# A planned attention-and-GLU kernel on one core: dummy key products in TensorE's rests, three head groups' row sums moved to VectorE, and new order tables

## The chip, the cores and the metric

The kernel runs on one core of a Trainium2 chip. The metric is device time in microseconds of the whole program; of several runs the median counts. One further execution was profiled, and everything below that is called the profile or the trace comes from it.

## The reference

Sequence length 2048, width 1024, 32 query heads of width 32 that share one key head and one value head, and a gated feed-forward part of width 3584. All tensors are bfloat16.

```python
x = A_x
h = x + attention(layernorm(x))       # q = xn@wq (32 heads), k = xn@wk, v = xn@wv (one head)
                                      # softmax(q k^T / sqrt(32)) v, heads side by side, @ wo
g, u = layernorm(h) @ w_gate, layernorm(h) @ w_up
out = h + (sigmoid(g) * u) @ w_down
```

## The kernel before

**Attention.** Scores are made in 512 *bursts* of four matmuls (L846 `s_burst`). Each of the four uses another 32-row strip of TensorE's array, so the four run at once; together they write 128 keys x 2048 query-head columns into four banks of PSUM (`S_ps`, three pairs of banks). ScalarE reads each half of a burst with one exponential (L866, 1024 columns, 1024 of them in the program) and writes it to a ring of tiles in SBUF (`Pr`; at first also to columns of `QT` and to `wo`, which are free then). Burst k may start when exponential 2k-2 has left its bank. Eight bursts cover 1024 keys for one query tile of 128 rows and 16 heads, and are a *group* (g). Two groups make all 2048 keys, and four groups make a query tile. The first 64 bursts (8 groups, tiles 0 and 1) are the *head*: meanwhile the layer norm of all 16 tiles, their transposes (DMA, L599) and the products for k, v and q are still being made.

For each group TensorE multiplies the probabilities with V (L953 `pv_group`, eight slots of four matmuls on 32-column strips) into one of only two banks, `X_ps`. The row sums of a group come in one of two ways (`SUM_PLAN`). With "p", TensorE multiplies all eight tiles with ones (L1015, eight slots). With "d", VectorE first adds the tiles pairwise (L903, L915: 14 adds of 128x1024), and TensorE multiplies only the sum with ones (L1000, one slot). Groups 0 to 7 have a letter each in `SUM_PLAN`; later groups are "d", only the last two bursts of all are added by L1015. Then VectorE transposes, inverts and multiplies (L1048 to L1058), which gives the attention output of the tile.

**The rest.** `wo_group` (projection and residual), second layer norm, and then the feed-forward part in eight *units* of two tiles: gate and up products (weights streamed from HBM in halves of 512 KB by SyncE's queue), a tanh on ScalarE (L1280) for the sigmoid, their product on VectorE (L1302), and the down products (`zone,hact` in the rows) with `w_down` kept in SBUF. Unit c runs while the scores of later tiles run; the last unit has nothing left to run beside.

**Three ways to use the array.** A product outside the scores is issued either as one matmul on all 128 columns (L368, mode "f") or as four at once on 32-column strips (L370, mode "pv"). Scores use row strips (mode "s"). In the rows below `128*128`, `128*32` and `32*128` are the three modes. `by_columns` chooses between "f" and "pv" for a product so as to keep the mode that the array is in; it refuses "pv" when too many instructions (`I_MAX`) were issued in the last 4 us.

**What sets the order.** All instructions of all engines are written by one Python loop, once, before launch. It keeps a clock for each engine (`k_pe`, `k_dve`, ...), adds estimated costs to it, and issues the next burst as soon as its clock says that the exponential is done (`due`), and otherwise products: of `todo` (k, v and the first q), `q_list`, `wo_list`, `ffn_list`, and P V groups by the letters of `PV_PLAN`. When nothing is ready it moves the clock on by 0.02 to 0.05 us and looks again; on the chip TensorE then waits at its next instruction. The tables (`TODO`, `PV_PLAN`, `Q_PLAN`, `LN_LEAD`, ...) steer these choices; they move instructions but do not change what is computed. The clock's estimates are not used for any time in this document.

```python
def run_item(g):                              # one product of a group
    if g.bank is None:
        ...
        need(pe, *after)                      # TensorE waits for the operands
        open_group(g)                         # and for one of the two X_ps banks
    mode("pv" if g.kind == "f" and by_columns(g) else g.kind)

def s_burst(k):
    g, b = BURST[k]
    t, i = ORDER[g]
    mode("s")
    need(pe, (c_e, 2 * k - 1) if k > 0 else None, *s_ready(k), ...)

def spare_dve():                              # may a q product of q_list or Q2 be started?
    return len(xn_val) >= min(NT, int(LN_LEAD + LN_RATE * k[0]))
```

Of the kernel before, what the change touches and what calls it, by code (L numbers as in the profile page):

```python
# [12 lines left out]
P = 128  # L13
# [73 lines left out]
def bass_sequential_preLN__grouped_kv_mqa__glu_gated_glu__prompt_kernel(  # L87
# [18 lines left out]
    NQ = D // P  # L106
# [13 lines left out]
    U_PLAN = "56391274"  # L120
    PV_PLAN = "aDcBBBaaDAaAeaabaDaAabaaaBaBDaaaabaDbbaaaAaAAcAaaBaAaaAaBCbDBadbaEDaDDaB"
    WO_PLAN = "aabbbaab"
    PV_HOLD = 1.5
# [3 lines left out]
    LN_LEAD = 1  # L127
    LN_RATE = 0.35
    T_PLAN = "aaadadad"
    H_ROOM = 0.2  # L130
    Q_PLAN = "daadddddddddddddddddddadddddddad"
# [22 lines left out]
    WD_FROM, WD_GAP, WD_LATE = 10, 6, 12  # L154
# [5 lines left out]
    QREC = 32  # L160
    QORD = 0
    URG0 = 0
    K_ACT = 1
# [5 lines left out]
    with ExitStack() as es:  # L169
# [99 lines left out]
        def _(unused):  # L269
# [33 lines left out]
            for i in range(2, 4):  # L303
                load_wq(i, 256 * i, 256)
                load_x(i + 2)

# [44 lines left out]
            I_US, I_MAX = 4.0, 240  # L351
# [37 lines left out]

            def run_item(g):  # L390
                if g.bank is None:
# [446 lines left out]
            def s_burst(k):  # L838
                g, b = BURST[k]
                t, i = ORDER[g]  # L840
                mode("s")
# [637 lines left out]
            wv_val = dma(act, wv, A_wv.rearrange("(a p) j -> p a j", p=P), d_w[1], 200)  # L1479
            need(dve, wk_val)  # L1480
# [34 lines left out]
            q_list += [(q, 512, 512) for q in range(NQ)]  # L1515
# [3 lines left out]
            for x in TODO:  # L1519
                if x[0] == "k":  # L1520
                    todo.append(("k", [int(y, 16) for y in x[1:]]))
                elif x[0] == "C":
                    todo.append(("C", int(x[1])))
                elif x[0] == "v":
                    todo.append(("v", int(x[1])))
                elif x[0] == "q":
                    i = "abcd".index(x[2])
                    todo.append(("q", int(x[1]), [2 * i, 2 * i + 1]))
                elif x == "Q2":
                    todo += [("Q", q, QC, QC) for q in range(NQ)]  # L1530
# [65 lines left out]
            while True:  # L1596
# [52 lines left out]
                if busy(pv[0]):  # L1649
                    t_ = pv[0].items[0][2]()  # L1650
                    if t_ > k_pe[0] + 0.02:
# [14 lines left out]
                if busy(urg[0]):  # L1666
# [5 lines left out]
                    else:  # L1672
                        k_pe[0] += 0.02
# [25 lines left out]
                if busy(cur[0]):  # L1699
                    if cur[0].bank is None and k_pe[0] + 0.02 < min(bank_time(b) for b in range(2)) < k_pe[0] + 3.0:  # L1700
                        k_pe[0] += 0.02
# [7 lines left out]
                if (pv_follow[0] is None and pv_next[0] < NCH and kk > LAST_K[pv_next[0] - 1] + 2 and blocked()  # L1709
# [3 lines left out]
                    continue  # L1713
                k_pe[0] += 0.05
# [36 lines left out]
```

## Time and profile before

| | |
|---|---|
| runs | 1095.84, 1095.35, 1093.97 us; median 1095.35 |
| the profiled execution | 1094.13 us, of it span 1092.4 us (1.73 us lie around the span) |
| mean granted TensorE clock | 0.998 |
| TensorE busy | 1069.2 us, 98% of the span |
| ScalarE busy | 1004.1 us, 92% |
| VectorE busy | 871.3 us, 80% |

The span is long and even: the first 12 us bring the first tile to its scores, bursts run from 12 us to 1008 us, and 84 us follow the last burst. A busy share of 98% on TensorE says little alone, since matmuls are pipelined and a record lasts longer than the time until the next can start; so the prediction uses the distance from start to start. Of 14650 matmuls in the program 14595 have a record in the trace.

### The profile page before, as it was taken

To read this page: it belongs to the slowest core of one execution; us is meant where nothing else is said; L and a number is where in the kernel's file an instruction comes from. 1 tells how busy PE (TensorE), PEld (TensorE's weight loads), DVE (VectorE), ACT (ScalarE), POOL (GpSimd) and SP (SyncE) were. 2 spreads that over 40 slices of the span, in tenths; PEclk is the share of its full clock that TensorE was granted. 3 is DMA by queue.
4 is the path that set the end of the run, shared out by engine and by line. 5 is a ranking of instruction groups with operands and counts; after the bars stand their busy time and mean duration, and the time that the engine had idled before them with its cause. 6 is when DMAs were issued, how large, how long until landed. Compare 5 with 4: busy or idle time off the path is not lost. (4 is left out here: it accounts for less than half of the span.)

```text
span 1092.4 us, 33342 instructions
## 1 busy us (share of the span) xinstructions
PE 1069.2 (98%) x14595; PEld 615.1 (56%) x14648; DVE 871.3 (80%) x1439; ACT 1004.1 (92%) x1151; POOL 63.7 (6%) x135
## 2 busy tenths in 40 slices
PE   8899999999999999999999999999999999999999
PEld 6433356644666356643666447653666447653884
DVE  7864578898988989799988988798988989888321
ACT  6999999999999999999999999999999999999110
POOL 2321110000000000000000000000000000000000
PEclk9999999999999999999999999999999999999999
DMA  9646338841977449680988619771586519761570
GB/s 216 119 103 208 98 79 232 247 118 39 243 208 199 104 104 257 195 207 20 248 228 222 151 26 269 199 181 30 142 235 193 116 30 261 202 189 27 147 194 20
DMA packets 324433, 172.16 MB, mean 158 GB/s; under 512 B 39488, under 2 KB 318272, under 8 KB 324288
## 3 DMA queue, kind: packets, MB, share of 16 engines
q1 hardware_dynamic: 319472, 160.33, 57.9%
q0 software_dynamic: 2592, 9.44, 2.6%
q8 instruction: 115, 1.88, 0.7%
q10 hardware_dynamic: 2224, 0.26, 0.2%
q14 instruction: 30, 0.25, 0.1%
HBM read 157.94 MB, written 4.19 MB: 148 GB/s over the span
## 5 line engine op out<-in xcount | busy, mean ns | idle before, releaser
L866 ACT ACTIVATE Pr<-S_ps 128x1024 bf16<-128x1024 f32 x992 | 943.9, 1186 | 3.2 <-PE S_ps L846 2.7
L903 DVE TENSOR_TENSOR pairs<-Pr 128x1024 bf16<-128x1024 bf16 x446 | 303.5, 683 | 31.6 <-ACT Pr L866 31.1
L915 DVE TENSOR_TENSOR pairs<-pairs 128x1024 bf16<-128x1024 bf16 x390 | 269.1, 690 | 12.0
L846 PE MATMUL S_ps<-QT,kT 32*128 32x512 bf16 x2048 | 202.7, 385 | 6.3 <-ACT Pr L866 5.3
L368 PE MATMUL X_ps<-QT,wgu 128*128 128x128 bf16 (+1 forms) x2040 | 189.5, 243 | 0.2
L368 PEld LDWEIGHTS X_ps<-QT,wgu 128*128 128x128 bf16 x2040 | 148.3, 98 | 34.8 <-issue 23.6
L368 PE MATMUL X_ps<-zone,hact 128*128 128x512 bf16 (+2 forms) x680 | 156.6, 371 | 4.3 <-issue 4.0
L368 PE MATMUL X_ps<-QT 128*128 128x128 bf16 (+1 forms) x1550 | 145.3, 244 | 0.0
L846 PEld LDWEIGHTS S_ps<-QT,kT 32*128 32x128 bf16 x2048 | 51.6, 91 | 162.4 <-ACT Pr L866 143.9
L368 PEld LDWEIGHTS X_ps<-QT 128*128 128x128 bf16 x1550 | 114.5, 98 | 24.3 <-issue 15.2
L1280 ACT ACTIVATE gu<-X_ps 128x512 f32<-128x512 f32 x112 | 86.3, 771 | 44.9 <-PE X_ps L368 44.1
L953 PE MATMUL X_ps<-Pr,V 128*32 128x512 bf16 x1984 | 127.2, 381 | 0.1
L1302 DVE SCALAR_TENSOR_TENSOR hact<-gu,X_ps 128x512 bf16<-128x512 f32 x112 | 76.4, 682 | 48.1 <-PE X_ps L368 41.7
L368 PEld LDWEIGHTS X_ps<-zone,hact 128*128 128x128 bf16 x714 | 61.5, 98 | 77.3 <-issue 19.3
L953 PEld LDWEIGHTS X_ps<-Pr,V 128*32 128x32 bf16 x1984 | 46.4, 96 | 50.9 <-issue 13.8
L370 PE MATMUL X_ps<-QT,wgu 128*32 128x256 bf16 (+1 forms) x2400 | 72.5, 264 | 0.7 <-issue 0.6
L370 PEld LDWEIGHTS X_ps<-QT,wgu 128*32 128x32 bf16 x2400 | 57.5, 97 | 13.3 <-issue 7.9
L368 PE MATMUL X_ps<-zone 128*128 128x128 bf16 (+3 forms) x481 | 55.4, 261 | 2.3 <-DVE zone L557 1.3
L440 POOL CAST mean<-mv 128x1 f32<-128x1 bf16 x28 | 7.6, 271 | 823.4 <-DVE mv L1166 791.1
L370 PE MATMUL X_ps<-zone,hact 128*32 128x512 bf16 x840 | 55.5, 380 | 0.0
L368 PE MATMUL X_ps<-wo,QT 128*128 128x512 bf16 x198 | 50.3, 380 | 1.8 <-issue 1.3
L1340 DVE SCALAR_TENSOR_TENSOR hx<-X_ps,hx 128x512 bf16<-128x512 f32 (+2 forms) x33 | 22.2, 672 | 26.7 <-PE X_ps L368 25.6
(108 smaller groups left out, 623.5 us busy)
## 6 DMA issues: line engine op xcount, KB each, us to landing
wgu<-in_B_w_up_dram SPq DMA_DIRECT2D x80, 512.0 KB, 5.5
wgu<-in_B_w_gate_dram SPq DMA_DIRECT2D x72, 512.0 KB, 5.6
QT<-in_B_w_gate_dram SPq DMA_DIRECT2D x53, 512.0 KB, 5.2
QT<-in_B_w_up_dram SPq DMA_DIRECT2D x45, 512.0 KB, 5.6
zone<-in_B_w_down_dram POOLq DMA_DIRECT2D x14, 512.0 KB, 4.5
hx<-in_A_x_dram SPq DMA_DIRECT2D x17, 256.0 KB, 3.1
out_dram<-hx SPq DMA_DIRECT2D x31, 128.0 KB, 1.7
Pr<-in_B_w_gate_dram SPq DMA_DIRECT2D x5, 512.0 KB, 6.9
```

Source lines behind the costliest of these rows:

```text
L368: return pe.matmul(out, lhsT=lhsT, rhs=rhs, start=start, stop=stop, skip_group_check=main[0])
L370: ins = pe.matmul(out[DH * j:DH * (j + 1)], lhsT=lhsT[:, DH * j:DH * (j + 1)], rhs=rhs, start=start, stop=stop, tile_position=(0, DH * j), ...
L440: return c_pool.inc(pool.tensor_copy(out=mean[:, i:i + 1], in_=mv[:, i:i + 1, 0]), 0.2)
L846: ins = pe.matmul(S_ps[:, ((2 * k + j // 2) % 3) * 2 + j % 2, :], lhsT=kT4[DH * j:DH * (j + 1), kt * P:(kt + 1) * P], rhs=QT[DH * j:DH * ( ...
L866: c_e.inc(act.activation(out=p_tile(k, n % 2), in_=S_ps[:, 2 * pr:2 * pr + 2, :].rearrange("p a (b q) -> p (a b) q", q=QC), func=ACTF.Exp, ...
L903: slot_use[x] = c_dve.inc(dve.tensor_tensor(out=dst(x), in0=p_tile(k - 1, hh), in1=p_tile(k, hh), op=ALU.add), T_ADD, 0.08)
L915: slot_use[x] = slot_use[y] = c_dve.inc(dve.tensor_tensor(out=pairs[:, x, :], in0=pairs[:, x, :], in1=pairs[:, y, :], op=ALU.add), T_ADD, ...
L953: ins = pe.matmul(bank[DH * j:DH * (j + 1), :], lhsT=V[:, kt, :], rhs=p_tile(kx, j // 2)[:, j % 2 * 2:j % 2 * 2 + 2, :], start=b == bs[0], ...
L1280: tanh_val[n] = c_act.inc(act.activation(out=slot, in_=bank, func=ACTF.Tanh, scale=0.5), T_TANH, 0.1)
L1302: gu_read[n] = c_dve.inc(dve.scalar_tensor_tensor(out=hact[:, 2 * fs[0]:2 * fs[0] + ft, r0:r0 + len(ts) * P], in0=slot.rearrange("p (a b) ...
L1340: v = c_dve.inc(dve.scalar_tensor_tensor(out=hv, in0=bank[:, 0:n], scalar=0.5, in1=hv, op0=ALU.mult, op1=ALU.add), 0.03 + n * 0.00113, 0.08)
```

## The change

Tables and constants change, and four pieces of code:

- `fill()` is new. Whenever the loop moves TensorE's clock on for want of work it notes the start of the rest; at the next product or burst, `fill` puts dummy products (128x128, a key tile with itself, into a free `X_ps` bank that nobody reads) into the rest if at least seven fit.
- `SUM_PLAN` turns groups 4, 5 and 6 of the head from "p" to "d".
- `TODO` could now hold "Q4", by which the queries of tiles 4 to 7 would be made in two halves; the new `TODO` holds "Q2" and no "Q4", so these queries are made as before.
- The loop is told landing times for the first loads (`.at[16] = ...`); this alters its clock alone.

`I_MAX` 240 to 180 makes `by_columns` refuse "pv" sooner; `PV_HOLD` 1.5 to 0 no longer lets a P V group delay a burst; `LN_LEAD` 1 to 4 holds q products back until more tiles are normalized; `QREC` 32 to 24 frees the upper columns of `QT` sooner; `WD_FROM`, `WD_LATE` shift the loads of `w_down` on GpSimd's queue.

```diff
-    PV_PLAN = "aDcBBBaaDAaAeaabaDaAabaaaBaBDaaaabaDbbaaaAaAAcAaaBaAaaAaBCbDBadbaEDaDDaB"
+    PV_PLAN = "bbabdaaaEabeEaBadddabaEaAaaABaBabBaBbaEaaBAAaBabaaaBaDaaabaDabaabaEedEEa"
-    PV_HOLD = 1.5
+    PV_HOLD = 0
-    LN_LEAD = 1
+    LN_LEAD = 4
-    SUM_PLAN = "pppppppp"
+    SUM_PLAN = "ppppdddp"
-    TODO = ["C1", "q1a", "q0c", "v1", "Q2", "q1b", "k3", "q0d", "C3", "q1d", "v5", "k1", "C2", "v7", "v2", "k2",
-            "v0", "v3", "q1c", "v6", "v4"]
+    TODO = ["v5", "Q2", "q1b", "q1a", "k2", "v3", "q1d", "q0c", "C1", "v0", "C3", "v6", "v2", "v4", "C2", "v7",
+            "k3", "v1", "q0d", "k1", "q1c"]
...
-    WD_FROM, WD_GAP, WD_LATE = 10, 6, 12
+    WD_FROM, WD_GAP, WD_LATE = 30, 6, 14
-    QREC = 32
+    QREC = 24
-    K_ACT = 1
+    K_ACT = 3
...
+            for i, t_ in enumerate((6.2, 9.1, 12.3, 15.5)):
+                d_w[2 + i].at[16] = t_
...
-            I_US, I_MAX = 4.0, 240
+            I_US, I_MAX = 4.0, 180
...
+            rest = [None]
+            def fill():
+                t, rest[0] = rest[0], None
+                n = 0 if t is None or k[0] >= NB else int((k_pe[0] - t - (0.2 if pe_mode[0] == "f" else 0.3)) / 0.058)
+                if n < 7:
+                    return
+                free = [b for b in range(2) if bank_free[b] != "open" and bank_time(b) <= t + 0.1]
+                if not free:
+                    return
+                f = bank_free[free[0]]
+                need(pe, f(True) if callable(f) else f)
+                pe_mode[0] = "f"
+                for i in range(n):
+                    pe.matmul(X_ps[:, free[0], 0:P], lhsT=kT4[:, 0:P], rhs=kT4[:, 0:P], start=True, stop=True,
+                              skip_group_check=True)
+                count[0] += 2 * n
...
-            q_list += [(q, 512, 512) for q in range(NQ)]
+            q_list += [(q, 768, 256) if "Q4" in TODO else (q, 512, 512) for q in range(NQ)]
...
+                        rest[0] = k_pe[0] if rest[0] is None else rest[0]
                         k_pe[0] += 0.05
```

Line numbers rise by up to 25 in the changed kernel: scores are L871 there, "f" products L373, "pv" products L375, P V L978, sums of added tiles L1025, row sums by ones L1040, dummies L409.

**Where instructions move.** On TensorE, in the head, bursts 9 to 12. Before, bursts stand there without a product between two of them (a row with `x8` is two bursts in a row), and no dummy exists:

```order
L846 MATMUL S_ps<-QT,kT 128x512 x4
L368 MATMUL X_ps<-zone 128x256 x8
L368 MATMUL X_ps<-zone 128x32 x16
L846 MATMUL S_ps<-QT,kT 128x512 x8
L664 MATMUL X_ps<-zone 32x128 x32
L846 MATMUL S_ps<-QT,kT 128x512 x4
```

Now bursts 5 to 7, where `X_ps<-kT` are the dummies:

```order
L373 MATMUL X_ps<-zone 128x128 x10
L373 MATMUL X_ps<-zone 128x32 x12
L871 MATMUL S_ps<-QT,kT 128x512 x4
L373 MATMUL X_ps<-zone 128x32 x4
L409 MATMUL X_ps<-kT 128x128 x18
L871 MATMUL S_ps<-QT,kT 128x512 x4
L409 MATMUL X_ps<-kT 128x128 x20
L871 MATMUL S_ps<-QT,kT 128x512 x4
L373 MATMUL X_ps<-zone 128x256 x10
```

The dummies stand ahead of bursts 6 and 7 (counted from 0); seven more stand in unit 0, ahead of burst 103. The double burst, 10 and 11, is gone. On TensorE, in the second half of the head (bursts 48 to 51), before:

```order
L846 MATMUL S_ps<-QT,kT 128x512 x4
L370 MATMUL X_ps<-zone 32x512 x4
L953 MATMUL X_ps<-Pr,V 32x512 x32
L1015 MATMUL X_ps<-Pr,ones 32x512 x4
L846 MATMUL S_ps<-QT,kT 128x512 x4
L1015 MATMUL X_ps<-Pr,ones 32x512 x28
L846 MATMUL S_ps<-QT,kT 128x512 x4
```

and now:

```order
L871 MATMUL S_ps<-QT,kT 128x512 x4
L375 MATMUL X_ps<-zone 32x512 x16
L978 MATMUL X_ps<-Pr,V 32x512 x20
L871 MATMUL S_ps<-QT,kT 128x512 x4
L978 MATMUL X_ps<-Pr,V 32x512 x12
L375 MATMUL X_ps<-zone 32x512 x16
L871 MATMUL S_ps<-QT,kT 128x512 x4
```

The eight slots of row sums are gone, and the P V group is shared out over two bursts. On TensorE, from the last burst on, before:

```order
L846 MATMUL S_ps<-QT,kT 128x512 x4
L370 MATMUL X_ps<-zone,hact 32x512 x8
L953 MATMUL X_ps<-Pr,V 32x512 x4
L370 MATMUL X_ps<-zone,hact 32x512 x28
L953 MATMUL X_ps<-Pr,V 32x512 x4
L370 MATMUL X_ps<-zone,hact 32x512 x16
L1000 MATMUL X_ps<-pairs,ones 32x512 x4
L1015 MATMUL X_ps<-Pr,ones 32x512 x8
L368 MATMUL X_ps<-QT,wgu 128x128 x32
L368 MATMUL X_ps<-QT 128x128 x15
L368 MATMUL X_ps<-wo,QT 128x512 x8
```

and now:

```order
L871 MATMUL S_ps<-QT,kT 128x512 x4
L978 MATMUL X_ps<-Pr,V 32x512 x28
L375 MATMUL X_ps<-zone,hact 32x512 x16
L978 MATMUL X_ps<-Pr,V 32x512 x4
L375 MATMUL X_ps<-zone,hact 32x512 x20
L1025 MATMUL X_ps<-pairs,ones 32x512 x4
L1040 MATMUL X_ps<-Pr,ones 32x512 x8
L373 MATMUL X_ps<-zone,hact 128x512 x8
L373 MATMUL X_ps<-QT 128x128 x16
L373 MATMUL X_ps<-QT,wgu 128x128 x16
L373 MATMUL X_ps<-wo,QT 128x512 x16
```

Six P V slots and four slots of down products have moved from ahead of the last burst to behind it; the gate and up products behind the last burst are as many as before.

More of the change, by code (lines that the diff above doesn't have):

```diff
@@ L119, in bass_sequential_preLN__grouped_kv_mqa__glu_gated_glu__prompt_kernel @@
     NGU = 4
-    U_PLAN = "56391274"
-    PV_PLAN = "aDcBBBaaDAaAeaabaDaAabaaaBaBDaaaabaDbbaaaAaAAcAaaBaAaaAaBCbDBadbaEDaDDaB"
-    WO_PLAN = "aabbbaab"
-    PV_HOLD = 1.5
+    U_PLAN = "75601517"
+    PV_PLAN = "bbabdaaaEabeEaBadddabaEaAaaABaBabBaBbaEaaBAAaBabaaaBaDaaabaDabaabaEedEEa"
+    WO_PLAN = "aababaaa"
+    PV_HOLD = 0
     BANK_WAIT = 0.1
@@ L126, in bass_sequential_preLN__grouped_kv_mqa__glu_gated_glu__prompt_kernel @@
     G_SUM, HCH, HB0 = 4, 4, 2
-    LN_LEAD = 1
+    LN_LEAD = 4
     LN_RATE = 0.35
-    T_PLAN = "aaadadad"
+    T_PLAN = "aaaddadd"
     H_ROOM = 0.2
-    Q_PLAN = "daadddddddddddddddddddadddddddad"
-    SUM_PLAN = "pppppppp"
+    Q_PLAN = "dadddddddddaddddddddddaddddddddd"
+    SUM_PLAN = "ppppdddp"
     HOLD0 = 2
     K_BUSY = 10
-    TODO = ["C1", "q1a", "q0c", "v1", "Q2", "q1b", "k3", "q0d", "C3", "q1d", "v5", "k1", "C2", "v7", "v2", "k2",
-            "v0", "v3", "q1c", "v6", "v4"]
+    TODO = ["v5", "Q2", "q1b", "q1a", "k2", "v3", "q1d", "q0c", "C1", "v0", "C3", "v6", "v2", "v4", "C2", "v7",
+            "k3", "v1", "q0d", "k1", "q1c"]
     ORDER = [(0, 0), (1, 0), (0, 2), (1, 2), (0, 1), (0, 3), (1, 1), (1, 3)]
@@ L305, in _ @@
                 load_x(i + 2)
+            for i, t_ in enumerate((6.2, 9.1, 12.3, 15.5)):
+                d_w[2 + i].at[16] = t_
+            for i, t_ in enumerate((3.8, 7.2, 9.8, 10.5, 13.0, 17.2)):
+                d_x[i].at[16] = t_
+            d_w[0].at[16], d_x0.at[16] = 7.3, 3.6
             warm = pairs[:, 1, 0:256]
@@ L840, in s_burst @@
                 t, i = ORDER[g]
+                fill()
                 mode("s")
@@ L1479, in _ @@
             wv_val = dma(act, wv, A_wv.rearrange("(a p) j -> p a j", p=P), d_w[1], 200)
+            d_w[1].at[16] = 15.2
             need(dve, wk_val)
@@ L1528, in _ @@
                     todo.append(("q", int(x[1]), [2 * i, 2 * i + 1]))
-                elif x == "Q2":
-                    todo += [("Q", q, QC, QC) for q in range(NQ)]
+                elif x[0] == "Q":
+                    todo += [("Q", q, int(x[1]) // 2 * QC, QC) for q in range(NQ)]
             def spare_dve():
@@ L1672, in _ @@
                     else:
+                        rest[0] = k_pe[0] if rest[0] is None else rest[0]
                         k_pe[0] += 0.02
@@ L1700, in _ @@
                     if cur[0].bank is None and k_pe[0] + 0.02 < min(bank_time(b) for b in range(2)) < k_pe[0] + 3.0:
+                        rest[0] = k_pe[0] if rest[0] is None else rest[0]
                         k_pe[0] += 0.02
@@ L1713, in _ @@
                     continue
+                rest[0] = k_pe[0] if rest[0] is None else rest[0]
                 k_pe[0] += 0.05
```

1 line of the change is left out of this document (added).

## The prediction

> **What bounds the kernel now.** I read the page's busy times first, then busy time by stretches of 16 bursts, then TensorE's and ScalarE's instructions in order of time at the places where a stretch is longer than its work.
>
> ```profile
> span 1092.4 us, 33342 instructions
> PE 1069.2 (98%) x14595; PEld 615.1 (56%) x14648; DVE 871.3 (80%) x1439; ACT 1004.1 (92%) x1151; POOL 63.7 (6%) x135
> ```
>
> The stretches begin and end with bursts 0, 16, 32, 48, 64, 80, 96; then come bursts 96 to 128, one whole unit (192 to 256), and what follows the last burst. Columns: stretch and its length, busy time (and instructions) of each engine, granted clock, DMA.
>
> ```profile
> 12.10:45.70 33.60, 29.44 (x425) 18.63 (x424) 28.25 (x72) 31.06 (x38) 12.52 (x30) 0.95 0.84 164
> 45.70:74.80 29.10, 28.13 (x474) 11.47 (x470) 22.51 (x46) 29.10 (x33) 8.17 (x21) 1.00 0.30 54
> 74.80:104.90 30.10, 28.89 (x354) 11.23 (x352) 13.71 (x22) 29.92 (x33) 4.55 (x6) 1.00 0.86 249
> 104.90:135.80 30.90, 30.85 (x295) 11.45 (x295) 15.57 (x25) 30.00 (x34) 5.07 (x9) 1.00 0.29 86
> 135.80:168.60 32.80, 31.73 (x510) 19.91 (x510) 25.32 (x42) 31.72 (x37) 2.88 (x6) 1.00 0.40 95
> 168.60:201.10 32.50, 32.43 (x573) 22.03 (x571) 27.74 (x46) 32.50 (x40) 2.17 (x3) 1.00 0.85 241
> 201.10:262.20 61.10, 60.23 (x689) 28.84 (x694) 53.99 (x87) 61.06 (x69) 3.28 (x6) 1.00 0.50 132
> 387.10:511.60 124.50, 123.20 (x1713) 70.08 (x1719) 109.21 (x176) 124.49 (x143) 3.40 (x7) 1.00 0.66 170
> 1008.30:1092.40 84.10, 81.61 (x873) 62.37 (x872) 20.33 (x33) 10.71 (x17) 1.29 (x3) 1.00 0.46 118
> ```
>
> The reader is to see that in a unit ScalarE is busy 124.49 of 124.50 us and TensorE 123.20: two engines end together, and saving on one alone shortens nothing. ScalarE has visible holes only in the head: 2.54 us to 45.70, then 0, 0.18, 0.90 and 1.08. Behind the last burst TensorE alone counts.
>
> ScalarE's pace, and the price of its holes (length of the row, xcount, idle time before it):
>
> ```profile
> 40.69 5.65 ACT L866 ACTIVATE Pr<-S_ps 128x1024 bf16<-128x1024 f32 x6 [0.84 <-PE S_ps L846]
> 123.50 12.97 ACT L866 ACTIVATE Pr<-S_ps 128x1024 bf16<-128x1024 f32 x14 [0.66 <-PE S_ps L846]
> 161.29 1.02 ACT L866 ACTIVATE Pr<-S_ps 128x1024 bf16<-128x1024 f32 x1 [0.62 <-PE S_ps L846]
> 184.11 0.82 ACT L1280 ACTIVATE gu<-X_ps 128x512 f32<-128x512 f32 x1
> 184.59 2.17 ACT L866 ACTIVATE Pr<-S_ps 128x1024 bf16<-128x1024 f32 x2
> 186.39 0.86 ACT L1280 ACTIVATE gu<-X_ps 128x512 f32<-128x512 f32 x1
> 301.81 0.60 ACT L1280 ACTIVATE gu<-X_ps 128x512 f32<-128x512 f32 x1 [0.75 <-PE X_ps L370]
> ```
>
> Fourteen exponentials take 12.97 us and one 1.02, so in a long run one follows the other after (12.97-1.02)/13 = 0.919 us, 1.84 a burst; two between two tanhs take only (186.39-184.59)/2 = 0.90 each. A tanh costs 184.59-184.11 = 0.48.
>
> TensorE's prices, from start to start:
>
> ```profile
> 991.42 0.39 PE L846 MATMUL S_ps<-QT,kT 32*128 32x512 bf16 x4
> 991.75 1.47 PE L368 MATMUL X_ps<-zone,hact 128*128 128x512 bf16 x6
> 993.15 0.40 PE L846 MATMUL S_ps<-QT,kT 32*128 32x512 bf16 x4
> 1033.43 3.74 PE L368 MATMUL X_ps<-QT 128*128 128x128 bf16 x64
> 1037.89 15.88 PE L368 MATMUL X_ps<-QT,Pr 128*128 128x256 bf16 x144
> ```
>
> x64 of 128 columns advance by (3.74-0.22)/63 = 0.056 us, x144 of 256 by 0.109; x6 of 512 take 1.47, the last about 0.39 long, so (1.47-0.39)/5 = 0.216. Six of them would let the next burst start after 1.30, and it starts after 1.40: a change of array mode costs 0.10, and 0.33-0.22 = 0.11 on the way back.
>
> **The change, part by part.** Counts come from the programs' order.
>
> *Row sums.* Groups 4 to 6 lose 24 slots of ones and gain 3 sums: 21 x 0.216 = 4.5 us less on TensorE. VectorE gains 42 adds, about 14 a group.
>
> ```profile
> L903 DVE TENSOR_TENSOR pairs<-Pr 128x1024 bf16<-128x1024 bf16 x446 | 303.5, 683 | 31.6 <-ACT Pr L866 31.1
> 104.91 0.39 PE L846 MATMUL S_ps<-QT,kT 32*128 32x512 bf16 x4
> 105.46 1.90 PE L953 MATMUL X_ps<-Pr,V 128*32 128x512 bf16 x32
> 107.51 0.40 PE L846 MATMUL S_ps<-QT,kT 32*128 32x512 bf16 x4
> 107.83 1.70 PE L1015 MATMUL X_ps<-Pr,ones 128*32 128x512 bf16 x28
> 109.46 0.40 PE L846 MATMUL S_ps<-QT,kT 32*128 32x512 bf16 x4
> ```
>
> 42 x 0.683 = 29 us on VectorE lie between 75 and 136 us, where it is busy 13.71 of 30.10 and 15.57 of 30.90, so 32 us are free: it just fits, since the sums may wait behind products. Were that cover gone, P V groups would wait for ring tiles; I bound this by 0 and 1.4 us, the longest wait of TensorE in the rests below. What is gained is not 4.5: before burst 48 a stretch stands at ScalarE's pace (32 x 0.919 = 29.4 of 30.10), where I take 0. From 104.90 TensorE is the later one (busy 30.85 of 30.90; bursts 2.60 us apart at 107.51, against 1.84). Slots and mode changes there fall from 30.8 to 29.4, and ScalarE's 29.4 plus a 0.5 us cast becomes the bound: 30.9 to 29.9, **-1.0**.
>
> *Bursts 64 to 80.* One wait of TensorE ends with a transpose's landing, and ScalarE's hole at 161.29 follows it:
>
> ```profile
> 158.29 0.89 PE L368 MATMUL X_ps<-QT,zone 128*128 128x128 bf16 x13
> 160.19 0.73 PE L368 MATMUL X_ps<-QT,zone 128*128 128x128 bf16 x10 [1.02 <-DMA QT<-hn]
> ```
>
> TensorE's work falls from 31.4 to 30.8 (0.9 us of q products are left behind burst 64 instead of 3.5). ScalarE needs 29.4 + 4 x 0.48 + 0.5 = 31.8 of 32.80. I take all of it, **-1.0**; bounds -1.1 (all holes) and +1.0 (the transpose is as late and nothing covers it).
>
> *Rests and dummies.* The head's rests of TensorE:
>
> ```profile
> 33.49 0.40 PE L846 MATMUL S_ps<-QT,kT 32*128 32x512 bf16 x4
> 35.31 0.40 PE L846 MATMUL S_ps<-QT,kT 32*128 32x512 bf16 x4 [1.42 <-ACT Pr L866]
> 36.91 0.63 PE L664 MATMUL X_ps<-zone 128*32 128x128 bf16 x32 [1.21 <-DMA zone<-hn]
> 37.81 2.30 PE L368 MATMUL X_ps<-zone 128*128 128x32 bf16 x20
> 40.04 0.61 PE L846 MATMUL S_ps<-QT,kT 32*128 32x512 bf16 x4
> ```
>
> After 2.6 us of rest the clock of the stretch is 0.95, twenty matmuls of 32 columns take 2.30 us, the burst at 40.04 comes 2.56 us after the one before, and ScalarE idles 0.84. 45 dummies (2.5 us) are issued, 38 of them ahead of bursts 6 and 7, where the loop now rests. If they keep the clock, the 0.84 goes: **-0.8**. They cost nothing while the rest outlasts them; a rest that does not come makes them cost up to 38 x 0.056 = 2.1. What queues behind them is the burst and with it ScalarE. The Trainium skill (TensorE: Matmul & The Clock Gate, "Why this matters for your kernels") asks only that no idle gap exceed about 3 us; by that neither rest would slow the clock, the dummies would be worth nothing and the sum 0.8 higher. This trace disagrees: 1.42 and 1.21 sufficed.
>
> *Fewer products on column strips.* 904 fewer matmuls on column strips are issued. ScalarE's longest hole in a unit, 0.75 at 301.81, ends with such a product (L370). With fewer of them I take **-0.6**; bounds 0 and -0.8.
>
> *Mode changes.* 1026 become 1062, of them 20 more between bursts 128 and 511: 2.1 us. Slots there fall by 2.4 (ten of them, 2.2, are moved behind the last burst), so TensorE's load per unit stays: **-0.3**. The bounds are wider, since the two engines are level there and any displaced product tells: a unit has 128 x 0.90 + 14 x 0.48 = 121.9 of exponentials and tanhs, 2.6 under its 124.5. A fifth of that more or less in each of six units is 3 us either way.
>
> *Behind the last burst.* Ten more slots, 2.2 us; in return the stall ahead of `wo` goes, since 3.5 us of products now cover the normalization:
>
> ```profile
> 1008.29 0.39 PE L846 MATMUL S_ps<-QT,kT 32*128 32x512 bf16 x4
> 1014.66 1.00 PE L368 MATMUL X_ps<-QT 128*128 128x128 bf16 x15
> 1015.82 1.67 PE L368 MATMUL X_ps<-wo,QT 128*128 128x512 bf16 x7 [0.16 <-issue]
> ```
>
> 15 x 0.056 = 0.84 of the 1.16 between two starts is work, 0.3 is stall. **+1.9**; this lies fully on the path.
>
> *At nothing.* The halved queries do not occur. Three more of the `w_down` loads now stand ahead of the first second-layer-norm steps on GpSimd's queue, but `wo` of tile 0 comes six bursts later too, and the first down product stays at burst 110, over 40 bursts later. If a load waits ahead of that norm, tile 0's gate products wait too, and 0.9 us of q products is all that is left to cover it; I take 0, with A's bound. The new K_ACT and T_PLAN letters leave ScalarE's small casts at 14.
>
> Sum: -1.0 -1.0 -0.8 -0.6 -0.3 +1.9 = -1.8, from 1094.13 to 1092.3. The profiled execution lies 1.2 below the median of the runs; I add half of that: **1092.9**.
>
> **The rivals.** A measurement of this kernel can tell about 0.2% (2.2 us) from no change.
>
> *A: the end grows and the head gives nothing.* In the first stretch the change puts 4 and 2 more products ahead of bursts 1 and 2 and holds q products back until four tiles are normalized. If TensorE then rests longer than the dummies last by bursts 6 to 9, ScalarE idles there as it does at 40.69, twice 0.84, and the clock's 0.8 is lost as well. Then the last burst starts no earlier than 1008.3 plus 0 to 1.7, and the end adds 1.9: 1095.35 + 1.9 to 3.6, about 1098. It decides from a last burst later than 1008.6. For it: ScalarE is full in every unit, so nothing is caught up later. Against: in the head its holes sum to 4.7 us.
>
> *B: TensorE's own sum decides.* The Trainium skill (TensorEngine Tiling (Array Packing), "Key Properties") states that changing the tiling mode drains the engine; the rows agree with 0.10 to 0.11 each, and this speaks against the change. If TensorE were the later engine everywhere: slots -4.5 -0.2 (fewer 128-wide) +2.5 (dummies) and 36 x 0.105 = +3.8, together +1.6 with dummies exposed and -0.9 with them hidden: 1094.5 to 1097, no change. Against: from 12 to 262 us TensorE's scores wait for exponentials, so it has time to spare there:
>
> ```profile
> PE S_ps L846 <- ACT Pr L866: 3.4, 4, 1.4
> ```
>
> *C: the units get shorter.* No P V group may delay a burst any more (`PV_HOLD` 0). If that brings the units a quarter of the way to their 121.9, 0.65 us each, six give -4 on top: 1089. Against: P V groups still stand whole between two bursts in 12 places, against 15.
>
> **How the numbers follow.** My forecast 0.37, A 0.28, B 0.27, C 0.08. Faster by over 0.2% (under 1093.2): the forecast and C, 0.45; within: B, 0.27; slower (over 1097.5): A, 0.28. The range runs from C's 1089 to A's 1098.5; the widest bounds of a single cost, 3 us either way of 1092.9, lie inside.
>
> **What would show it.** Right: clock 1.00 in the first 50 us; bursts 48 to 64 in about 29.9 us and 64 to 80 in 31.8; the last burst near 1004.5 and 86.0 us behind it. Wrong: holes of ScalarE of over 1 us at bursts 6 to 16, TensorE waiting for `pairs` of groups 4 to 6, or units longer than 124.5.

## The result, and the profile after

The changed kernel takes 1089.24 us (median of 6 runs, 1088.99 to 1089.72) against 1095.59 of the kernel before in the same comparison (6 runs, 1093.97 to 1096.75): a ratio of 0.9945, 95% interval 0.9933 to 0.9958. Two later comparisons gave 1089.16 against 1093.47 (0.9962, 0.9949 to 0.9976) and 1089.11 against 1092.74 (0.9963, 0.9950 to 0.9977). The kernel after stays within 0.2 us; it is the kernel before that wanders from one comparison to the next. So the change is worth 3.6 to 6.4 us, 0.4 to 0.6%. The forecast of 1092.9 had the sign right and was 3.7 too high; the measured time lies 0.2 above the lower end of the stated range.

The two profiled executions differ by 4.6 us (1094.13 and 1089.49). The busy times of the page after:

```profile
span 1087.8 us, 31948 instructions
PE 1069.5 (98%) x13878; PEld 612.5 (56%) x13930; DVE 896.4 (82%) x1481; ACT 1001.9 (92%) x1151; POOL 64.0 (6%) x135
```

TensorE is as busy as before and ScalarE nearly so (1004.1 before); the span is shorter. Busy time by stretches of the kernel after (bursts 0 to 16, 48 to 64, 64 to 80, one unit from burst 192 to 256, behind the last burst), columns as in the prediction:

```profile
12.30:44.30 32.00, 29.74 (x464) 20.32 (x462) 26.34 (x69) 30.55 (x38) 11.07 (x26) 1.00 0.77 154
103.70:133.40 29.70, 29.66 (x391) 11.02 (x390) 26.07 (x43) 29.70 (x34) 5.12 (x9) 1.00 0.31 91
133.40:164.70 31.30, 31.15 (x522) 20.45 (x519) 29.23 (x50) 31.30 (x37) 3.22 (x5) 1.00 0.44 120
382.60:506.70 124.10, 122.82 (x1554) 69.35 (x1561) 109.15 (x176) 124.10 (x143) 3.41 (x7) 1.00 0.64 171
1001.90:1087.80 85.90, 83.40 (x888) 63.49 (x888) 20.68 (x34) 10.85 (x17) 1.29 (x3) 1.00 0.46 116
```

The clock of the first stretch is 1.00 instead of 0.95, ScalarE is busy throughout the next two shown, VectorE has taken the adds (26.07 of 29.70 instead of 15.57 of 30.90), and the end has grown. All stretches, in us, read from the first instruction of the bursts in both traces:

| bursts | before | after | difference |
|---|---|---|---|
| ahead of burst 0 | 12.05 | 12.31 | +0.26 |
| 0 to 16 | 33.66 | 32.03 | -1.62 |
| 16 to 48 | 59.20 | 59.35 | +0.15 |
| 48 to 64 | 30.93 | 29.73 | -1.20 |
| 64 to 80 | 32.78 | 31.32 | -1.46 |
| 80 to 128 | 93.57 | 93.20 | -0.36 |
| 128 to 511, six units | 746.10 | 743.93 | -2.16 |
| behind the last burst | 84.11 | 85.87 | +1.76 |

To see what a gap between two bursts is made of, I count TensorE's work in it from the order (0.216 us a slot of 512 columns, 0.109 of 256, 0.056 of 128, 0.025 of 32, 0.103 a mode change) and call what is left of its length TensorE's rest:

| bursts | work before | rest before | work after | rest after |
|---|---|---|---|---|
| 0 to 16 (after: dummies counted as work) | 26.6 | 7.0 | 28.6 | 3.4 |
| 48 to 64 | 30.7 | 0.2 | 29.3 | 0.4 |
| 64 to 128 | 123.5 | 2.8 | 122.0 | 2.5 |
| 128 to 511 | 732.6 | 13.5 | 732.3 | 11.6 |

In the six units work falls by only 0.3; it is the rest that shrinks, from 326 gaps of 383 with under 0.03 us of it to 353. ScalarE shows the same 2 us from its side, though its busy share hides them: the record of an exponential lasts 1.19 us on average (before), while the next one can start 0.904 us after it. Counted from start to start, the exponentials between bursts 128 and 511 lose 13.7 us over that pace before and 11.2 after. TensorE's waits for exponentials between bursts 128 and 511, before and then after (us, times, longest):

```profile
PE S_ps L846 <- ACT Pr L866: 1.9, 7, 0.5
```

```profile
PE S_ps L871 <- ACT Pr L891: 0.4, 1, 0.4
```

### The profile page after: what moved, and what is told of

The parts are those of the page before. It is cut to its first block, busy times and chain, and to the rows that moved or that the text cites. A ratio compares the mean times of both kernels' runs of the same rounds, so it can differ in the third digit from the quotient of the medians.

```text
span 1087.8 us, 31948 instructions
## 1 busy us (share of the span) xinstructions
PE 1069.5 (98%) x13878; PEld 612.5 (56%) x13930; DVE 896.4 (82%) x1481; ACT 1001.9 (92%) x1151; POOL 64.0 (6%) x135
## 4 chain that ended last, share of the span: by engine, by line
PE 66%; ACT 4%; issue 1%; DVE 1%; ACTq 0%
PE X_ps L373 40%; PE S_ps L871 10%; PE X_ps L375 8%; PE X_ps L978 7%; ACT Pr L891 3%; PE X_ps L1025 1%; ACT gu L1305 1%; DVE pairs L928 0%; DVE pairs L940 0%; DVE olp L994 0%; DVE hact L1327 0%; PE X_ps L1040 0%; DVE hx L1365 0%; ACTq L46 0%
## 5 line engine op out<-in xcount | busy, mean ns | idle before, releaser
L928 DVE TENSOR_TENSOR pairs<-Pr 128x1024 bf16<-128x1024 bf16 x470 | 320.0, 682 | 27.4 <-ACT Pr L891 26.8
L940 DVE TENSOR_TENSOR pairs<-pairs 128x1024 bf16<-128x1024 bf16 x408 | 281.6, 690 | 12.0
L373 PE MATMUL X_ps<-QT,wgu 128*128 128x256 bf16 (+1 forms) x2235 | 215.7, 246 | 0.7 <-DMA QT<-hn 0.7
L871 PE MATMUL S_ps<-QT,kT 32*128 32x512 bf16 x2048 | 202.0, 385 | 2.4 <-ACT Pr L891 1.1
L373 PEld LDWEIGHTS X_ps<-QT,wgu 128*128 128x128 bf16 x2235 | 167.3, 98 | 40.6 <-issue 26.1
L373 PE MATMUL X_ps<-zone,hact 128*128 128x512 bf16 (+2 forms) x650 | 149.4, 371 | 4.4 <-issue 4.0
L373 PE MATMUL X_ps<-QT 128*128 128x128 bf16 (+1 forms) x1550 | 150.3, 246 | 0.0
L871 PEld LDWEIGHTS S_ps<-QT,kT 32*128 32x128 bf16 x2048 | 51.4, 91 | 156.9 <-ACT Pr L891 141.4
L373 PEld LDWEIGHTS X_ps<-QT 128*128 128x128 bf16 x1550 | 115.8, 98 | 25.1 <-issue 16.2
L978 PE MATMUL X_ps<-Pr,V 128*32 128x512 bf16 x1984 | 127.6, 381 | 0.4
L373 PEld LDWEIGHTS X_ps<-zone,hact 128*128 128x128 bf16 x685 | 59.1, 98 | 73.9 <-issue 18.6
L978 PEld LDWEIGHTS X_ps<-Pr,V 128*32 128x32 bf16 x1984 | 46.3, 96 | 51.8 <-issue 13.1
L375 PE MATMUL X_ps<-zone,hact 128*32 128x512 bf16 x956 | 61.9, 380 | 0.0
L373 PE MATMUL X_ps<-wo,QT 128*128 128x512 bf16 x208 | 53.5, 380 | 1.3 <-issue 0.6
L373 PE MATMUL X_ps<-zone 128*128 128x128 bf16 (+3 forms) x461 | 49.8, 253 | 2.6 <-DMA zone<-hn 1.1
L375 PE MATMUL X_ps<-QT,wgu 128*32 128x256 bf16 (+1 forms) x1428 | 46.9, 265 | 0.9 <-DVE olp L994 0.9
L375 PEld LDWEIGHTS X_ps<-QT,wgu 128*32 128x32 bf16 x1428 | 33.2, 96 | 12.7 <-issue 7.5
```

The lines of the kernel that those rows point to most:

```text
L373: return pe.matmul(out, lhsT=lhsT, rhs=rhs, start=start, stop=stop, skip_group_check=main[0])
L375: ins = pe.matmul(out[DH * j:DH * (j + 1)], lhsT=lhsT[:, DH * j:DH * (j + 1)], rhs=rhs, start=start, stop=stop, tile_position=(0, DH * j), ...
L871: ins = pe.matmul(S_ps[:, ((2 * k + j // 2) % 3) * 2 + j % 2, :], lhsT=kT4[DH * j:DH * (j + 1), kt * P:(kt + 1) * P], rhs=QT[DH * j:DH * ( ...
L928: slot_use[x] = c_dve.inc(dve.tensor_tensor(out=dst(x), in0=p_tile(k - 1, hh), in1=p_tile(k, hh), op=ALU.add), T_ADD, 0.08)
L940: slot_use[x] = slot_use[y] = c_dve.inc(dve.tensor_tensor(out=pairs[:, x, :], in0=pairs[:, x, :], in1=pairs[:, y, :], op=ALU.add), T_ADD, ...
L978: ins = pe.matmul(bank[DH * j:DH * (j + 1), :], lhsT=V[:, kt, :], rhs=p_tile(kx, j // 2)[:, j % 2 * 2:j % 2 * 2 + 2, :], start=b == bs[0], ...
```

## The experiments

My theory after the result: in the head the dummies keep the clock, the row sums' cost is TensorE's work in the gap where it stands, and in the units both engines are at their limit, so that work added to either tells and work taken from one does not. The rivals: TensorE's sum alone decides (rival B of the prediction), or ScalarE's alone. Unless said otherwise a kernel keeps the order of the kernel after, instruction by instruction, so stretches can be compared at 0.2 us; medians are set against 1089.1 to 1089.2.

**The dummies left out.**

```diff
-                for i in range(n):
-                    pe.matmul(X_ps[:, free[0], 0:P], lhsT=kT4[:, 0:P], rhs=kT4[:, 0:P], ...)
```

> The kernel after with its 45 dummy products left out and everything else in the same order on every engine. Theory D (the dummies keep TensorE's clock through the rests of the head): the granted clock of the stretch from burst 0 to burst 16 falls from 1.00 to about 0.95, ScalarE's holes there grow from 1.45 us to about 2.3, and the time is 0.8 us longer, up to 1.6; if the clock's drop comes in some runs and not in others, the runs also spread wider than the 0.7 us of the kernel after, nearer to the 2.8 us of the kernel before. Rival O (the order of the head made the gain, the dummies nothing): clock 1.00, the stretch of 32.0 us stays within 0.3, the time too. The Trainium skill (TensorE: Matmul & The Clock Gate, Why this matters for your kernels) puts the limit at an idle gap of about 3 us, and by that O would hold.

1090.05 (6 runs, 1089.31 to 1090.77): +0.9. The first stretch of its trace; TensorE alone where its clock is down (length, busy, granted clock, DMA), of this trace and then of the kernel before; TensorE ahead of bursts 6 and 7 and behind them; and then the same place of the kernel after:

```profile
11.90:45.80 33.90, 29.86 (x427) 19.36 (x424) 26.54 (x69) 31.04 (x38) 10.97 (x26) 0.90 0.76 150
```

```profile
26.00:32.00 6.00, 4.99 (x26) 0.50 0.82 206
```

```profile
38.00:41.00 3.00, 3.00 (x31) 0.50 0.62 47
```

```profile
22.83 0.91 PE L373 MATMUL X_ps<-zone 128*128 128x128 bf16 x20 [1.04 <-DMA zone<-hn]
...
25.27 0.40 PE L868 MATMUL S_ps<-QT,kT 32*128 32x512 bf16 x4 [1.01 <-ACT wo L888]
27.01 0.61 PE L868 MATMUL S_ps<-QT,kT 32*128 32x512 bf16 x4 [1.34 <-ACT wo L888]
...
29.80 0.61 PE L868 MATMUL S_ps<-QT,kT 32*128 32x512 bf16 x4
30.35 2.68 PE L373 MATMUL X_ps<-zone 128*128 128x256 bf16 x13
```

```profile
25.65 0.40 PE L871 MATMUL S_ps<-QT,kT 32*128 32x512 bf16 x4
25.98 1.29 PE L409 MATMUL X_ps<-kT 128*128 128x128 bf16 x20
27.45 0.39 PE L871 MATMUL S_ps<-QT,kT 32*128 32x512 bf16 x4 [0.18 <-ACT wo L891]
...
29.29 0.39 PE L871 MATMUL S_ps<-QT,kT 32*128 32x512 bf16 x4 [0.24 <-ACT wo L891]
29.61 1.59 PE L373 MATMUL X_ps<-zone 128*128 128x256 bf16 x13
```

Without dummies TensorE rests 1.04, 1.01 and 1.34 us within 5 us; from 27 us on the same matmuls take longer (thirteen of 256 columns 2.68 instead of 1.59, a burst 0.61 instead of 0.39), the clock of the stretch is 0.90, since it is 0.50 for about 6 us (in the kernel before for about 3), and bursts 8 and 9 come 2.8 and 3.2 us after the ones before. The stretch takes 33.9 instead of 32.0, the last burst comes at 1003.1 instead of 1001.3 to 1001.9. Theory D holds on the clock; its guess on the spread does not (1.5 us, and the kernel after itself spread by 1.3 to 1.6 in the later comparisons). The trace is of the slowest of the six runs: three have a mean clock of 0.997 (1090.05 to 1090.77), three of 0.998 (1089.31 to 1090.05), so the 1.9 us of this stretch are more than the median shows. Nor do the dummies keep the clock in every run: of 16 runs of the kernel after two have a mean clock of 0.998, and these two take 1090.46 and 1090.20. The Trainium skill (TensorE: Matmul & The Clock Gate, "Why this matters for your kernels") asks for no idle gap above about 3 us; here the longest rest of the place was 1.34, so this trace disagrees.

**The dummies alone, in the order of before.**

```diff
+            def fill():
+                ...
             def run_item(g):
+                fill()
```

> The kernel before, its order untouched, with the 63 dummy products that the new rule puts into its rests before bursts 0 to 20 of the planner. Theory D: the clock of the stretch from burst 0 to burst 16 rises from 0.95 to 1.00, the burst that came 2.56 us after the one before comes after about 2, ScalarE's holes there fall by 0.8, the median falls by 0.8 to 1.6 from 1095.6, and the runs spread by less than 1 us instead of 2.8. Rival O: the stretch stays at 33.6 within 0.3, and so does the time. Rival B (dummies are work): if the rests are shorter than the dummies last, the time is longer by up to 63 x 0.056 = 3.5 us.

1093.05 (11 runs, 1091.63 to 1095.17) against 1093.62: a ratio of 0.9992, 0.9983 to 1.0001. The first stretch:

```profile
12.00:44.70 32.70, 31.23 (x476) 21.27 (x474) 28.24 (x72) 30.90 (x38) 12.77 (x30) 1.00 0.78 170
```

The clock is kept, in all 11 runs (mean clock 1.000; of 22 runs of before in that comparison 15 have 0.997 or 0.998), and the stretch, in which 50 of the 63 dummies stand, falls by 0.9. In the median that is 0.6, which the interval does not tell from nothing; but the runs of before agree with it. Their median is 1093.86 for the 15 with the lower clock and 1093.00 for the 7 with 1.000, so a run with the lower clock takes about 0.9 more, and 15 of 22 are such. The spread stays at 3.5, so the clock is only a part of what makes the kernel before wander; what the rest is, stays open. One more thing shows in this trace: in the same order bursts 64 to 80 take 31.8 instead of the 32.8 of before's trace, without the wait for the transpose there, and bursts 80 to 96 take 33.8 instead of 32.5.

**The row sums' slots put back.**

```diff
-                    for j in range(4):
+                    for j in [0, 1, 2, 3] * (8 if 4 <= g <= 6 else 1):
                         ins = pe.matmul(bank[DH * j:DH * (j + 1), :], lhsT=ones[:], ...)
```

> The kernel after with the product that makes the row sums of each of groups 4 to 6 made eight times instead of once, at the same place: 21 slots of 0.216 us, 4.5 us of TensorE's work, come back, VectorE's adds stay, the order is otherwise the same. By the prediction's step (TensorE is the later engine only from burst 48 on): bursts 32 to 48 stay within 0.3 us of 29.6, bursts 48 to 64 go from 29.7 to about 30.7, the time +1.0 to +1.3. Rival S (ScalarE alone bounds here, the row sums brought nothing): under +0.3. Rival B (TensorE's sum decides throughout): +4.5.

1092.84 (11 runs): +3.7 of 4.5 added. Bursts 32 to 48 take 30.8 instead of 29.6, bursts 48 to 64 32.7 instead of 29.7. TensorE and ScalarE at the second of the three places:

```profile
113.23 1.90 PE L1025 MATMUL X_ps<-pairs,ones 128*32 128x512 bf16 x32
114.95 0.82 PE L375 MATMUL X_ps<-zone 128*32 128x512 bf16 x12
115.70 0.39 PE L871 MATMUL S_ps<-QT,kT 32*128 32x512 bf16 x4
```

```profile
116.14 3.88 ACT L891 ACTIVATE Pr<-S_ps 128x1024 bf16<-128x1024 f32 x4 [1.31 <-PE S_ps L871]
```

A gap that is already full does not take seven slots more: the next burst comes 3.2 us after the last, ScalarE stands for 1.31, and about 1.4 of each 1.51 us added is lost. That is nearer to rival B than to the prediction's step, also ahead of burst 48, where I had taken 0. In the kernel before, the planner had put the same slots into gaps that held less: taking them away, together with the new order, brought 0.4 in bursts 32 to 48 and 1.2 in bursts 48 to 64, not 3.7.

**More work for TensorE in the units.**

```diff
-                    for j in range(4):
+                    for j in [0, 1, 2, 3] * (3 if g >= 2 * G_SUM else 1):
```

> The kernel after with the product that makes the row sums of groups 8 and later made three times instead of once: 28 sums, 56 slots of 0.216 us, 12.1 us more work for TensorE spread evenly from burst 64 to the last, about 1.7 us a unit, nothing else moved. Theory S (ScalarE sets the units' pace, TensorE catches up in its waits for exponentials): the units take 0 to 0.4 us more each, the time +0 to +3. Rival B (TensorE's own sum decides the units): +1.7 a unit, +12 in all. If both engines are level and every displaced product tells, as the prediction said: about half, +6.

1099.12 (5 runs): +9.9 of 12.1. The units grow by 1.2 to 1.6 us; the one from burst 192 to 256:

```profile
384.00:509.60 125.60, 124.35 (x1582) 70.21 (x1589) 109.22 (x176) 124.97 (x143) 3.40 (x7) 1.00 0.65 169
```

Between bursts 128 and 511 work grows by 10.4 and TensorE's rest falls by 1.6. Theory S is out: ScalarE's pace does not hide it.

**More work for ScalarE in the units.**

```diff
+                if n % 16 == 15 and k >= 64:
+                    act.activation(out=nmean[:, 0:1], in_=ones[:, 0:1], func=ACTF.Copy)
```

> The kernel after with one small copy of a 128x1 tile put behind every eighth burst's second exponential on ScalarE, from burst 64 on: 56 instructions, 8 a unit, nothing else moved; their own duration is read from the trace. Theory T (TensorE is the later engine in the units, as tripled sums suggested, where 1.73 us of its work a unit cost 1.4 to 1.6): ScalarE catches up, the units grow by less than a third of what the copies last. Theory L (both engines are level, whichever is displaced tells): the units grow by at least 80% of it, as with TensorE's work. Theory S (ScalarE alone sets the pace): all of it, but then the tripled sums would have been hidden.

1093.37 (11 runs): +4.2. In the trace an exponential behind a copy starts 0.996 us after the one ahead of it instead of 0.904, so 56 copies are 5.2 us, and 0.8 of it tells, as with TensorE. The units grow by 0.6 to 0.7 of 0.74. Theory L holds.

**Less work for ScalarE in the units.**

```diff
-                c_e.inc(act.activation(out=p_tile(k, n % 2),
+                less = QC // 4 if n % 16 == 15 and k >= 64 else 0
+                c_e.inc(act.activation(out=p_tile(k, n % 2)[:, :, 0:QC - less],
```

> The kernel after with a quarter of the columns left out of every sixteenth exponential from burst 64 on (the last 64 of each 256 queries; what stood in the tile stays there): 56 exponentials of 128x768 instead of 128x1024, nothing moved. At the own pace of 0.904 us for 1024 columns each is about 0.21 shorter, 12 us in all, 1.7 a unit. Theory L (both engines are at their limit in the units, so work taken from one alone brings little, though work added to either costs 0.8 of itself): the units shorten by less than 0.4 each, the time by less than 3. Theory S (ScalarE is the floor that stopped the saved mode changes from showing): by 1.2 or more each, the time by 8 to 12.

1086.26 (5 runs): -2.9 of 12 (against the kernel after of the other comparisons; it was not run in this one). A shortened exponential is followed by the next after 0.69 us instead of 0.904, as announced. Between bursts 128 and 511 the time falls by 1.8 us, 0.1 to 0.5 a unit. The kernel's busy time by ScalarE's forms and the unit from burst 192 to 256:

```profile
L892 ACT ACTIVATE Pr<-S_ps 128x768 bf16<-128x768 f32 x56 | 50.4, 899 | 0.0
```

```profile
381.70:505.60 123.90, 123.49 (x1563) 69.38 (x1559) 109.08 (x176) 123.82 (x143) 3.40 (x7) 1.00 0.66 171
```

TensorE is then busy 123.49 of 123.90. Added work costs 0.8 of itself on either engine; taken away on ScalarE it brings a quarter.

**Strips issued whole.**

```diff
-                if pe_mode[0] != "pv":
+                if pe_mode[0] != "pv" or main[0]:
                     return pe.matmul(out, lhsT, rhs, start=start, stop=stop, ...)
```

> The kernel after with each product that it issues as four column strips issued as one full-array matmul instead, at the same place in the order: 959 slots of equal length and 2877 fewer instructions, but 116 more changes of array mode ahead of the last burst, 86 of them behind burst 128. At 0.105 us a change that is 12.2 us of TensorE's time, 1.5 a unit. If mode changes are work like any other on TensorE, and 0.85 of it tells as with the tripled sums: +10 us. If strips have a cost of their own beside the changes that they save (four weight loads where one would do), the time comes out lower than that, by up to what they cost. If ScalarE sets the pace and the changes hide in TensorE's waits: under +3. The Trainium skill (TensorEngine Tiling (Array Packing), Key Properties) says that a change of tiling mode drains the engine, without a figure.

1096.99 (6 runs): +7.8 for 116 mode changes, 0.067 each. Between bursts 128 and 511 86 changes, 8.9 us by their own price, make 6.0. That fits mode changes being work like any other, and the prediction had their sign right. That strips cost something of their own is neither shown nor excluded by the 2 us between 7.8 and 10.

**33 mode changes saved at fixed order.**

```diff
-                if pe_mode[0] != "pv":
+                if item[0] in WHOLE or pe_mode[0] != "pv" and item[0] not in STRIPS:
```

> The kernel after with the form of 193 products chosen anew at the same places of the order: where a column-strip step (P V, sums of ones) stands in a gap between two bursts, the products of that gap go as strips too (117), and where none stands there, they go whole (76). That saves 33 of the 1060 mode changes ahead of the last burst and changes no order, load or evacuation. By what whole products cost (116 changes, +7.8 us, so 0.067 us a change): -2.2 us, and at the full 0.105 a change -3.5. If TensorE's time were hidden behind ScalarE's in these gaps: within 0.5 of the kernel after. If strips had a price of their own: no gain, or slower.

1090.16 (5 runs) against 1089.11 of the kernel after in the same comparison: no gain, 1.0 more. Between bursts 128 and 511 work falls by 2.1 and TensorE's rest grows by 1.9 (11.4 to 13.3), and 743.7 becomes 743.5. The trace shows an example; TensorE from burst 146 to burst 148, first of the kernel after in the same comparison, then of this one:

```profile
292.57 0.39 PE L871 MATMUL S_ps<-QT,kT 32*128 32x512 bf16 x4
292.89 1.50 PE L375 MATMUL X_ps<-QT,wgu 128*32 128x256 bf16 x48
294.32 0.28 PE L373 MATMUL X_ps<-QT,wgu 128*128 128x256 bf16 x1
294.54 0.39 PE L871 MATMUL S_ps<-QT,kT 32*128 32x512 bf16 x4
294.86 0.40 PE L375 MATMUL X_ps<-QT,wgu 128*32 128x256 bf16 x8
295.19 1.38 PE L373 MATMUL X_ps<-QT,wgu 128*128 128x256 bf16 x11
296.41 0.38 PE L373 MATMUL X_ps<-QT 128*128 128x256 bf16 x2
296.73 0.39 PE L871 MATMUL S_ps<-QT,kT 32*128 32x512 bf16 x4
```

```profile
293.55 0.39 PE L889 MATMUL S_ps<-QT,kT 32*128 32x512 bf16 x4
293.88 1.59 PE L373 MATMUL X_ps<-QT,wgu 128*128 128x256 bf16 x13
295.40 0.39 PE L889 MATMUL S_ps<-QT,kT 32*128 32x512 bf16 x4
295.73 1.59 PE L373 MATMUL X_ps<-QT,wgu 128*128 128x256 bf16 x13
297.16 0.38 PE L373 MATMUL X_ps<-QT 128*128 128x256 bf16 x2
297.71 0.39 PE L889 MATMUL S_ps<-QT,kT 32*128 32x512 bf16 x4 [0.17 <-ACT Pr L909]
```

Each of the two gaps has one change less, and burst 147 comes 0.12 us earlier; TensorE then waits 0.17 us for an exponential ahead of burst 148, where it did not wait, and from burst 146 to burst 148 both kernels take 4.16 us. The loss is one place in the head, ahead of which 60 strips of 32 columns stand where there were 15 whole products:

```profile
80.38 0.66 PE L375 MATMUL X_ps<-zone 128*32 128x32 bf16 x60
81.01 0.40 PE L889 MATMUL S_ps<-QT,kT 32*128 32x512 bf16 x4
82.66 0.20 PE L375 MATMUL X_ps<-zone 128*32 128x32 bf16 x4 [1.26 <-issue]
```

TensorE waits 1.26 us there for nothing that the profile shows, and it does not in the kernel after. So the strips have a price at this place; what it is, I did not test. One candidate: from 78 to 84 us the DMA engines are busy throughout, and one packet of the instruction queue (0.02 MB) falls into this time; whether TensorE waited for its instructions, the trace does not say. This is the version that the counts pointed to, and it does not beat the kernel after.

**One number of the change alone, in before.**

```diff
-    PV_HOLD = 1.5
+    PV_HOLD = 0
```

> The kernel before with one number of the change alone, PV_HOLD 0 in place of 1.5: its planner then orders the units anew by itself. By the order, TensorE's slots ahead of the last burst fall from 870.6 to 854.8 us at the same 1024 mode changes, and 13.4 us of slots more stand behind the last burst. Theory T (TensorE decides the stretch before the last burst): that stretch shortens by 13 to 16, the end grows by 13.4, the time within 3 of the kernel before. Theory S (ScalarE's sum decides there): the stretch shortens by at most 3, and the time is 10 to 13 longer. Theory L (both level; ScalarE's 121.9 a unit is a floor 2.6 under what a unit takes): it shortens by about half, the time +5 to +8.

1111.97 (4 runs) against 1093.47: +18.5, more than any of the three theories gave. The end is as the order says:

```profile
1013.30:1110.60 97.30, 94.72 (x811) 66.78 (x811) 21.75 (x35) 10.71 (x17) 1.29 (x3) 1.00 0.41 105
```

97.3 instead of 84.1 for 13.4 us more of slots. The stretch ahead of the last burst does not shorten for 15.8 us less of work, it grows from 996.2 to 1001.4: TensorE's rest rises from 2.8 to 13.8 between bursts 64 and 128 and from 13.5 to 23.1 behind them. Of the 13.8, 11.6 lie in one place, between bursts 109 and 118; the row shows 15 us of it:

```profile
230.00:245.00 15.00, 9.14 (x69) 2.61 (x71) 13.01 (x22) 13.71 (x16) 0.80 (x1) 0.70 0.41 110
```

TensorE has run out of products there, rests, is granted a clock of 0.70, and ScalarE in turn stands twice, 1.3 us each time. So what was taken out of the gaps here came back as rest or worse, and what was put behind the last burst cost in full.

**I_MAX alone undone, in after.**

```diff
-            I_US, I_MAX = 4.0, 180
+            I_US, I_MAX = 4.0, 240
```

> The kernel after with one number of the change undone, I_MAX back at 240, so that its planner uses more strips (7564 matmuls on strips instead of 6320) and orders the units anew. By the order: 2.3 us of slots and 24 mode changes (2.5 us) less ahead of the last burst, 2.4 us of slots more behind it. If TensorE's work ahead of the last burst decides: -4.8 x 0.8 there and +2.4 at the end, about 1.5 faster than the kernel after. If ScalarE is the floor that moved work runs into, as with PV_HOLD alone: that stretch stays within 1 and the time is 1.5 to 2.5 longer.

1094.83 (11 runs): +5.7 (5.1 between the two traces; the traced run is the fastest of the 11). The end is 88.3 instead of 85.9, as the slots say. Between bursts 128 and 511 4.2 us less work (728.1) come with 5.9 more rest (17.2): 745.3 instead of 743.7; bursts 64 to 96 take 1.0 more. TensorE's waits for exponentials over the whole run, of this kernel and then of the kernel after in the same comparison:

```profile
PE S_ps L871 <- ACT Pr L891: 2.3, 6, 0.5
```

```profile
PE S_ps L871 <- ACT Pr L891: 1.1, 3, 0.5
```

The sign is the floor reading's, less work and no less time, but its price is not: the stretch ahead of the last burst grows by 2.6, not by under 1. And the waits that the profile lays to exponentials grow by only 1.2 of the 5.9 us; what the rest waits for is not shown.

**The kernel after again**, to compare with on the same chips.

> The kernel after once more, as the thing that the other runs are compared with on one chip. On the chip of the first comparison it was 6.4 us under the kernel before with runs that lay 0.7 us apart. If both hold here, the difference is 5.5 to 6.5 us and the spread under 1.5.

> The kernel after a third time, to compare these two with on one chip: 1089 to 1090 us, spread under 1.6.

The medians are 1089.16 and 1089.11, spreads 1.6 (expected under 1.5) and 1.3 us; the differences from before are 4.3 and 3.6, less than the 5.5 to 6.5 expected, because before was faster there. Two traces of the same kernel agree within 0.2 us in every stretch behind burst 16 but one (0.4).

## Why the prediction was right, and where its sizes were off

- **The row sums, -1.0: -1.2 measured.** Bursts 48 to 64 take 29.7 against the 29.9 announced; work falls from 30.7 to 29.3 as counted (30.8 to 29.4). The adds on VectorE fit: no wait of TensorE for `pairs` of groups 4 to 6 shows. How much of it the slots made and how much the new order of the same products, no run separates, since the one that put the slots back put them all into one gap a group.
- **Bursts 64 to 80, -1.0: -1.5.** ScalarE is busy 31.30 of 31.30; the floor of 31.8 was too high because I took 0.919 an exponential where they follow each other at 0.904 (32 x 0.015 = 0.5). That all of it belongs to the change is not shown: with the dummies alone, in before's order, the wait for the transpose is gone as well and the stretch is 1.0 shorter.
- **Rests and dummies, -0.8: -1.6 in the stretch of the two traces, about -0.9 in the medians.** The mechanism was right: without the dummies the clock falls, and the stretch of that trace takes 33.9. What the lost clock costs depends on how long it is down, 3 us in before's trace (the dummies there bring 0.9) and 6 us in the trace without dummies (1.9). One row was misread: the `x20` at 37.81 is sixteen matmuls of 32 columns, still at full speed, and four of 512 columns, which follow each other at 0.43 us instead of 0.22.
- **Fewer column strips, -0.6, and mode changes, -0.3: -2.2 in the six units together.** Their work fell by the 0.3 that I had counted. The other 1.9 are TensorE's rest. That the units get shorter is what rival C forecast, to which I gave 0.08 and 4 us, at half its price; that the time came out near C's 1089 is luck, since more than half of what was missing lay outside the units. The step that was off is the argument on the engines: I took it that the level of the two engines gave a displaced product 3 us of uncertainty either way, put its middle at nothing, and had no term for how evenly the gaps are filled. C's own reason is not shown: `PV_HOLD` alone did the opposite on before. Which of the tables evened the gaps out the runs cannot say, and none changed the evenness by itself, so that it made the gain is argued from the counts. The `I_MAX` run speaks for the strip limit only together with a new order.
- **Behind the last burst, +1.9: +1.8.** Ten slots cost what they last; with `PV_HOLD` alone 13.4 us of slots cost 13.2, with `I_MAX` 2.4 cost 2.4. The last burst was announced near 1004.5 and came at 1001.9.
- **From the profiled execution to the median, +0.6.** It went the other way: the kernel after has no such distance (1089.49 profiled, 1089.24 median). That is 0.9 us of the miss of 3.7 (0.6 taken the wrong way and 0.25). The rest, by the two traces, are the dummies' 0.8, the units' 1.3, 0.5 of bursts 64 to 80, 0.4 between bursts 80 and 128 that I had not touched, 0.2 of the row sums and 0.1 of the end, less 0.4 ahead of burst 0 and in bursts 16 to 48.
- **Rival A** is out: the last burst comes at 1001.9, and ScalarE's holes of bursts 6 to 16 are gone. **Rival B** had the right price for work that is added (0.8 of it, on TensorE) and the wrong one for work that is taken away: 2.1 us less brought 0.2.

## What to carry to other kernels

Where two engines end together, price the sides apart: here work added to one cost 0.8 of itself, and work taken from one came back mostly as rest. What gained went with a more even filling of the gaps between their handovers. So count, gap by gap, the work of the engine that feeds the other, and compare the gaps rather than the sums. Work moved behind the point from which one engine is alone cost what it lasts, and each of the two single numbers of the planner that were changed alone made its kernel slower.

## What the runs showed of the chip that was not expected

- Rests of TensorE of 1.04, 1.01 and 1.34 us within 5 us were followed by matmuls at about 0.6 of their speed over the next 6 us (thirteen of 256 columns in 2.68 us instead of 1.59), at a granted clock of 0.50; with 38 dummies of 128 columns in two of those rests the clock stayed at 1.00 in 14 of 16 runs.
- Sixty strips of 32 columns in 0.66 us were followed by a stall of 1.26 us that has no releaser in the profile, where the largest group of such stalls in that kernel (29) reaches 0.2 at most.
